# A gated linear attention with an MLP on one core: the start of its hand-kept order table written anew

## The chip, the core and the metric

One core of a Trainium2 chip runs the whole kernel. The metric is the device time of one execution in microseconds (us). The core has five instruction streams that matter here: PE (TensorE, matrix products into PSUM), ACT (ScalarE, table functions and copies), DVE (VectorE, elementwise work), POOL (GpSimd, elementwise work, and issuer of the two weight transfers) and SP (SyncE, issuer of all other transfers). Each stream runs its instructions in the order in which they were written down, and waits where an instruction needs something that isn't there yet.

## The reference

Four batches, eight heads, 768 steps, 48 channels a head. A complex decay per step and channel drives a state; only the real part of the state is read.

```python
mag = np.sqrt(a_re * a_re + a_im * a_im)
scale = np.minimum(mag, 0.999) / (mag + 1e-06)
a_re_n, a_im_n = (a_re * scale, a_im * scale)
for t in range(S):
    new_re = ar * S_re - ai * S_im          # ar, ai: a_re_n, a_im_n of step t
    new_im = ar * S_im + ai * S_re
    kv = np.einsum('bhd,bhe->bhde', k[:, :, t], v[:, :, t])
    S_re, S_im = (new_re + kv, new_im)
    y[:, :, t] = np.einsum('bhd,bhde->bhe', q[:, :, t], S_re)
...
x = np.ascontiguousarray(attn_out.transpose(0, 2, 1, 3)).reshape(B, S, H * D)   # 384 wide
mu = np.mean(x, axis=-1, keepdims=True)
var = np.mean((x - mu) ** 2, axis=-1, keepdims=True)
xn = (x - mu) / np.sqrt(var + 1e-06) * g_ln
ch = np.maximum(xn @ w_ch1, 0.0) @ w_ch2     # 384 -> 1536 -> 384
return (x + ch).astype(np.float32)
```

## The kernel before

**Tiling.** The 768 steps of a batch are cut into 6 chunks of 128 steps. Two chunks form a pair, so there are 12 pairs P (three a batch) and 24 chunks n. Most of what depends on the decays is done by pairs, the attention itself and the layer norm by chunks, the MLP by pairs again. Only pair 0 has its decay work cut into two halves of four heads (`0.0` and `0.1`).

**One pair's steps**, by the names that the table uses (P is the pair, n the chunk, the last figure a half or a chunk within the pair):
- loads on SP: `are`, `aim` (decays, `in_a_re_dram`, `in_a_im_dram`), `k`, `q`, `vf` (values). `v` is the conversion of `vf` (L414).
- magnitude and angle of the decays: `ln` and `iv` on ACT (logarithm and reciprocal, L459, L461), `r` = quotient (L463, a product), `r2` its square (L467), `u` (ACT, L473), `l` and `lc` (DVE, L477 and L480: the capped log magnitude), `th` (ACT, arctangent, L496).
- running sums over the steps by matrix products with triangles of ones: `dec` (L488) for the magnitude, `ph` (L503, L507) for the angle; `car` carries the angle to the next pair; `qt` (L532) adds a quarter turn. From them ACT makes `e` and `en` (exponentials, L492) and `sin` and `cos` (L525, L536 and, later in the table, L548 with `abs` on DVE).
- `ke` = k times en, `qe` = q times e (float32 inputs), then `ks` and `qs` = ke and qe times the sine and cosine. These four are products of two tensors; they are cut in halves when the `.1` half stands in the table, and else the `.0` does the whole 768 (1536 for ks and qs).
- by chunks: `kT`, `qT` transpose on PE (or by a DMA), `ksT`, `qsT` copy out of PSUM; `am` is the score product (L636), `atm` its masking on DVE, `gm` the new part of the state (L660), `G` the state, `y` the attention output in PSUM (L697 and L700).
- layer norm and MLP: `bn` (DVE, L707 and L708), `x` (the centred row, L714 or L717), `xr` (what ot adds, L724), `xtr` and `xT` (transpose on PE, copy), `rstd` (POOL: an addition L753 and a power L755), `mm1` (first layer, L767, three groups of two parts a pair), `relu` (L779), `mm2` (second layer, L791), `ot` (L807), `st` (store).

**Once only.** `wl.0` loads the first layer's weights through POOL's queue, with conversion to bfloat16 (L369); nine `wc.jb.ec` multiply them by minus the norm's gain on DVE (L385), and `mm1.P.jb` needs the three `wc` of its group and both `xT` of its pair. `wl.1` loads the second layer's (L371). Constants (`ue`, `uth`, `pick`, `mask`, `ident`, `pad`, `one` ...) are written at the start; `uec` and `uthc` (L336), which only pairs 9 to 11 use, as well. `warm` are matrix products of constants whose result nobody reads (L821 to L828).

**What sets the order.** Nothing is scheduled by the compiler. The string PLAN (L44 to L142) lists every operation as `name:engine`, and each engine issues in the table's order. A figure behind the engine is the PSUM bank (there are eight); an operation that gets a bank waits until the bank's last owner has been read. An `@name` behind a POOL operation adds a wait: it begins only when the DVE operation of that name has ended (`turns at the shared port` in Graph.run). The tables of ACT's functions are loaded where `tab` stands.

The places around the start, in words: ACT works on the decays of pairs 0 and 1, then makes the sines and cosines of pairs 0 and 1, last cos.1.0. DVE multiplies ke and qe by them in order; qs.1.0.0 is the last of this block. Then come the copies, masks, states and norms of chunks 0 to 3 with the transposes and products of PE between them, the nine `wc`, and `mm1.0.*`.

Of the kernel before, what the change touches and what calls it, by code (L numbers as in the profile page):

```python
# [44 lines left out]
ue:G are.0.0:S are.1.0:S are.0.1:S uth:V aim.0.0:S warm.w27:P0 pad.ks.2:G warm.1:P0 aim.0.1:S pad.qs.2:G warm.w1:P7  # L45
aim.1.0:S warm.w7:P0 tab.log.0:A ln.0.0:A pick:G@uth warm.w29:P5 are.2.0:S iv.0.0:A warm.w32:P0 car0.0:G warm.w10:P7
pad.qs.1:G ln.1.0:A warm.w35:P4 vf.0.0:S uec:G warm.w5:P7 ln.0.1:A pad.qs.0:G warm.22:P2 iv.1.0:A warm.10:P4 r.0.0:V
warm.6:P5 one:G zrow.1:G vf.0.1:S ident:G warm.w24:P5 iv.0.1:A warm.26:P7 warm.w26:P6 r.0.1:V warm.17:P6 gln:S
warm.21:P5 warm.18:P4 r.1.0:V warm.w15:P4 warm.24:P4 q.0.0:S warm.20:P3 warm.w25:P2 tab.trig.1:A th.0.0:A warm.w39:P3
# [5 lines left out]
q.1.0:S car.0.1:V0 en.0.1:A1 r.2.0:V qrow:G warm.w16:P2 en.0.0:A7 ph.1.0:P2 e.1.0:A4 q.2.1:S ke.0.0.0:V e.0.0:A7
warm.28:P1 are.3.0:S r2.2.0:V en.1.0:A4 warm.19:P7 warm.w4:P1 ke.0.1.0:V vf.1.0:S u.2.0:A warm.w0:P5 qe.0.0.0:V
warm.w40:P4 warm.w22:P7 car.1.0:V2 warm.w3:P7 k.1.0:S warm.5:P7 warm.w20:P5 l.2.0:V warm.w31:P7 warm.w23:P5 aim.3.0:S
warm.w21:P7 warm.w28:P1 qe.1.0.0:V tab.trig.3:A sin.0.1:A0 sin.0.0:A6 lc.2.0:V qt.0.1:P0 ks.0.1.1:V sin.1.0:A2 row.0:S
qs.0.1.1:V warm.w2:P7 warm.w19:P4 ks.0.0.1:V row.1:S qt.0.0:P6 qe.1.0.1:V cos.0.1:A0 qt.1.0:P2 vf.1.1:S cos.0.0:A6
# [5 lines left out]
bn.1:V5 decc.0:A4 xtr.0:P4 kT.3:P6 ksT.2:V7 ph.2.0:P2 G.1:V0 qe.2.0.1:G@ksT.2 tab.trig.5:A th.3.0:A ksT.3:V6 am.2:P0
ngl:G@ksT.2 sin.2.0:A2 warm.w37:P7 v.1:G atm.2:V0 warm.13:P7 am.3:P6 xT.0:A4 qt.2.0:P2 r2.3.0:G@ksT.3 x.1:A5 gm.2:P4
atm.3:V6 ph.3.0:P0 cos.2.0:A2 xr.0:G G.2:V4 warm.23:P2 are.5.0:S xtr.1:P2 car.3.0:A0 warm.9:P3 warm.w41:P6 sin.3.0:A0
gm.3:P4 wc.0.1:V y.2:P7 wc.1.0:V y.3:P5 xT.1:A2 wc.1.1:V wc.1.2:V vf.2.0:S qt.3.0:P0 wl.1:G@wc.1.1 bn.2:V7
mm1.0.1.0:P2 cos.3.0:A0 wc.0.0:V mm1.0.1.1:P2 vf.2.1:S wc.0.2:V x.2:A7 wc.2.2:V mm1.0.0.1:P0 wc.2.0:V relu.0.1:A2
wc.2.1:V bn.3:V5 mm1.0.0.0:P0 qe.2.0.0:G@wc.2.1 xtr.2:P3 aim.5.0:S x.3:V5 mm1.0.2.0:P6 ke.2.0.0:G@bn.3 xT.2:V3  # L70
xtr.3:P5 mm1.0.2.1:P6 xT.3:V5 tab.log.6:A u.3.0:A gs.3:V4 mm1.1.0.1:P2 qs.2.0.0:V relu.0.2:A6 mm1.1.1.0:P4 ks.2.0.0:V
relu.0.0:A0 mm1.1.1.1:P4 ks.2.0.1:V mm1.1.0.0:P2 l.3.0:V ln.4.0:A mm1.1.2.1:P0 relu.1.1:A4 relu.1.0:V2 kT.5:P6
mm1.1.2.0:P0 iv.4.0:A ksT.5:V6 qT.5:P4 relu.1.2:A0 lc.3.0:V qT.4:P3 r.4.0:G@ksT.5 qsT.5:V4 kT.4:P5 qsT.4:A3 dec.3.0:P6
ksT.4:V5 are.6.0:S am.5:P0 e.3.0:A6 rstd.0:G am.4:P2 atm.5:V0 r2.4.0:A mm2.0.0:P4 mm2.0.1:P4 atm.4:V2 u.4.0:A q.3.0:S
rstd.1:G@atm.5 mm2.2.0:P1 ln.5.0:A row.3:S mm2.0.2:P4 l.4.0:V q.3.1:S v.2:A mm2.2.1:P1 G.3:G ot.0:V4 mm2.2.2:P1
iv.5.0:A lc.4.0:V k.3.1:S gm.4:P5 en.3.0:A6 dec.4.0:P2 r.5.0:G G.4:V5 y.4:P4 oa.2:A1 st.0:S y.5:P0 bn.4:V4 mm2.3.0:P7
ln.6.0:A k.3.0:S ot.2:G bn.5:V0 mm2.1.0:P6 en.4.0:A2 x.4:V4 mm2.3.1:P7 e.4.0:A2 st.2:S r2.5.0:V vf.3.1:S mm2.1.1:P6
qe.3.0.0:V x.5:A0 row.4:S xtr.4:P2 qe.3.0.1:V iv.6.0:A mm2.3.2:P7 vf.3.0:S xr.3:G@qe.3.0.0 xT.4:V2 xtr.5:P5 u.5.0:A
mm2.1.2:P6 xr.1:G@qe.3.0.1 q.4.0:S xT.5:V5 ke.3.0.1:G ot.3:V7 mm1.2.0.0:P4 ot.1:V6 mm1.2.0.1:P4 aim.6.0:S rstd.2:G
qs.3.0.0:V k.4.0:S mm1.2.2.0:P2 tab.trig.7:A th.4.0:A ke.3.0.0:V mm1.2.2.1:P2 k.4.1:S relu.2.0:A4 ks.3.0.0:V ph.4.0:P6  # L80
st.1:S relu.2.2:A2 st.3:S l.5.0:V qT.6:P0 q.4.1:S abs.4.0:A6 dps.4:P1 kT.6:P5 v.3:G@ks.3.0.0 qsT.6:V0 mm1.2.1.0:P2
are.7.0:S th.5.0:A decc.4:V1 ksT.6:V5 kT.7:P0 sin.4.0:A6 vf.4.0:S dps.3:P4 mm1.2.1.1:P2 decc.3:V4 car.4.0:A6 ksT.7:V0
qT.7:P5 relu.2.1:A2 lc.5.0:V am.6:P6 r.6.0:G@ksT.7 qsT.7:V5 gm.6:P4 ph.5.0:P0 cos.4.0:A atm.6:V6 vf.4.1:S G.6:A4
am.7:P2 sin.5.0:A0 gm.7:P4 q.5.0:S ke.4.0.0:G@atm.6 atm.7:V2 y.6:P5 mm2.4.0:P7 abs.5.0:A0 ke.4.0.1:G mm2.5.0:P6
th.6.0:A G.7:V4 q.5.1:S y.7:P2 bn.6:V5 cos.5.0:A qe.4.0.0:G@G.7 mm2.5.1:P6 are.8.0:S bn.7:V2 x.6:A5 mm2.5.2:P6
aim.7.0:S x.7:V2 mm2.4.1:P7 ks.4.0.0:V k.5.1:S xtr.7:P2 xtr.6:P5 mm2.4.2:P7 tab.log.8:A ln.7.0:A xT.7:V2 ksT.8:S
dec.5.0:P0 xT.6:V5 r2.6.0:A qs.4.0.0:V kT.9:P4 e.5.0:A0 mm1.3.1.0:P2 v.4:G@xT.6 aim.8.0:S ksT.9:V4 en.5.0:A0 qT.8:P5
xr.5:V qe.5.0.0:G qT.9:P4 k.5.0:S qsT.8:V5 u.6.0:A mm1.3.1.1:P2 qsT.9:V4 rstd.3:G mm1.3.2.0:P0 relu.3.1:A2 l.6.0:V
am.9:P4 k.7.1:S mm1.3.2.1:P0 qe.5.0.1:G iv.7.0:A atm.9:V4 mm1.3.0.1:P2 relu.3.2:A0 xr.4:G@qsT.9 mm1.3.0.0:P2 lc.6.0:V
r.7.0:G ot.4:V7 ln.8.0:A dec.6.0:P4 ot.5:V6 relu.3.0:A2 gm.8:P7 st.5:S ph.6.0:P0 G.8:V7 st.4:S qs.5.0.0:V e.6.0:A4  # L90
k.6.1:S am.8:P2 vf.5.0:S mm2.6.0:P6 en.6.0:A4 r2.7.0:G@G.8 abs.6.0:V0 row.6:S mm2.6.1:P6 iv.8.0:A are.9.0:S car.6.0:V0
y.9:P4 atm.8:V2 u.7.0:A r.8.0:G@abs.6.0 qT.11:P5 gm.9:P7 mm2.6.2:P6 k.6.0:S bn.9:V4 y.8:P2 q.6.0:S gs.9:V7 mm2.7.0:P3
xr.6:G tab.trig.9:A sin.6.0:A0 bn.8:V2 G.9:G@gs.9 mm2.7.1:P3 x.9:A4 ot.6:V6 mm2.7.2:P3 x.8:A2 l.7.0:V st.6:S xtr.9:P7
th.7.0:A q.6.1:S qT.10:P4 qsT.11:V5 vf.5.1:S xtr.8:P6 xr.7:G@l.7.0 cos.6.0:A ph.7.0:P0 xT.8:V6 ke.5.0.0:G@qsT.11
xT.9:V7 th.8.0:A qsT.10:V4 dps.6:P2 mm1.4.1.0:P6 sin.7.0:A0 ot.7:V3 mm1.4.0.1:P4 st.7:S rstd.4:G decc.6:A2 ks.5.0.0:V
r2.8.0:A mm1.4.0.0:P4 k.7.0:S vf.6.1:S lc.7.0:V mm1.4.1.1:P6 ke.6.0.0:G relu.4.0:A4 car.7.0:V0 aim.9.0:S kT.10:P3
kT.11:P2 abs.7.0:A0 ksT.10:V3 mm1.4.2.0:P4 relu.4.1:A6 ksT.11:V2 q.7.0:S am.10:P0 ks.6.0.1:V dec.7.0:P2
ks.6.0.0:G@ksT.11 atm.10:V0 q.7.1:S am.11:P6 mm1.4.2.1:P4 atm.11:V6 tab.log.10:A en.7.0:A2 mm2.9.0:P1 v.5:G@atm.10
e.7.0:A2 mm2.9.1:P1 relu.4.2:V4 qe.6.0.0:G@atm.11 ln.9.0:A y.10:P0 row.7:S gm.10:P2 vf.7.0:S ph.8.0:P6 u.8.0:A
# [763 lines left out]
```

## Time and profile before

| | |
|---|---|
| median of 3 runs | 185.67 us (185.29 to 185.86) |
| profiled execution, own time | 185.77 us |
| its span | 184.1 us |
| busy in the span | PE 174.6, DVE 154.6, ACT 154.9, POOL 111.4 us |
| HBM | 28.31 MB read, 4.72 MB written, 179 GB/s over the span |

The profile is one execution. The span runs from the first instruction to the last; the execution's own time is 1.7 us longer, which lies around the span. PE busy means that matrix products are in flight, fillers among them. A timeline row gives start, duration, engine, line, operation, and output and input with their shapes; "x3" means that three instructions alike stand in one row, with the time of all three. A bracket gives the idle time ahead of it on its engine and who ended it. A row of the chain gives start, duration and what ran. A row of the table of stages gives the stretch, its length, and the busy time and count of each engine. "PEclk" is the granted clock of PE as a share of full speed, "DMA share" the mean busy share of the sixteen transfer engines.

### The profile page before, as it was taken

To read this page: it belongs to the slowest core of one execution; us is meant where nothing else is said; L and a number is where in the kernel's file an instruction comes from. 1 tells how busy PE (TensorE), PEld (TensorE's weight loads), DVE (VectorE), ACT (ScalarE), POOL (GpSimd) and SP (SyncE) were. 2 spreads that over 40 slices of the span, in tenths; PEclk is the share of its full clock that TensorE was granted. 3 is DMA by queue.
4 is the path that set the end of the run, shared out by engine and by line. 5 is a ranking of instruction groups with operands and counts; after the bars stand their busy time and mean duration, and the time that the engine had idled before them with its cause. 6 is when DMAs were issued, how large, how long until landed. Compare 5 with 4: busy or idle time off the path is not lost.

```text
span 184.1 us, 5013 instructions
## 1 busy us (share of the span) xinstructions
PE 174.6 (95%) x1971; PEld 137.8 (75%) x1971; DVE 154.6 (84%) x274; ACT 154.9 (84%) x217; POOL 111.4 (61%) x124
## 2 busy tenths in 40 slices
...
GB/s 156 306 195 240 231 194 198 197 246 207 241 178 149 263 244 228 210 204 198 184 239 155 253 203 217 221 171 196 151 199 177 200 152 190 230 184 89 109 0 85
DMA packets 128791, 35.39 MB, mean 192 GB/s; under 512 B 124800, under 2 KB 128000, under 8 KB 128768
## 3 DMA queue, kind: packets, MB, share of 16 engines
...
q8 instruction: 15, 0.25, 0.5%
...
HBM read 28.31 MB, written 4.72 MB: 179 GB/s over the span
## 4 chain that ended last, share of the span: by engine, by line
PE 74%; DVE 9%; SPq 6%; POOL 4%; issue 3%; DMA 2%; DVEq 0%; POOLq 0%
PE banks L767 24%; PE banks L791 24%; PE banks L613 6%; PE banks L636 5%; SPq L452 3%; PE banks L488 3%; PE banks L507 3%; PE banks L697 2%; DMA k<-in_k_dram 2%; SPq L404 2%; PE banks L660 2%; PE banks L700 2%; PE banks L734 2%; POOL ke L295 2%; PE banks L503 1%
## 5 line engine op out<-in xcount | busy, mean ns | idle before, releaser
L791 PE MATMUL banks<-w2b,h 128*128 128x384 bf16 (+2 forms) x300 | 53.0, 319 | 0.1
L767 PE MATMUL banks<-xT,w1b 128*128 128x256 bf16 x432 | 51.5, 273 | 0.0
L767 PEld LDWEIGHTS <-w1b 128*128 128x128 bf16 x432 | 46.1, 114 | 1.2 <-DVE stats L707 0.3
L779 ACT ACTIVATE h<-banks 128x1024 bf16<-128x1024 f32 x31 | 31.5, 1022 | 11.7 <-PE banks L767 11.3
L791 PEld LDWEIGHTS <-h 128*128 128x128 bf16 x300 | 26.9, 97 | 13.9 <-issue 0.2
L295 DVE TENSOR_TENSOR atm<-banks,mask 128x1024 bf16<-128x1024 f32 x24 | 28.9, 1220 | 3.5 <-PE banks L636 3.0
L295 POOL TENSOR_TENSOR r<-aim,are 128x768 f16<-128x768 f32 x9 | 16.5, 1832 | 8.6 <-DVE ksT L292 7.5
L831 ACT ACT_TABLE_LOAD x15 | 19.2, 1283 | 1.0 <-PEq L847 0.8
L295 POOL TENSOR_TENSOR qe<-q,e 128x384 bf16<-128x384 f32 (+1 forms) x14 | 16.2, 1156 | 4.7 <-ACT e L492 1.7
L826 PE MATMUL banks<-u_e 128*128 128x512 f16 x42 | 14.1, 424 | 2.4 <-POOL u_e L323 2.2
L724 POOL TENSOR_SCALAR xr<-x,mv 128x384 f32<-128x384 bf16 x13 | 8.5, 658 | 11.0 <-ACT x L714 4.5
L707 DVE BATCH_NORM_STATS2 stats<-banks 128x6 f32<-128x384 f32 x24 | 13.4, 556 | 1.4 <-PE banks L700 1.2
L636 PE MATMUL banks<-qsT,ksT 128*128 128x128 bf16 x192 | 14.3, 219 | 0.0
L807 DVE SCALAR_TENSOR_TENSOR ot<-banks,rstd,xr 128x384 f32<-128x384 f32 (+2 forms) x18 | 10.4, 587 | 3.9 <-PE banks L791 3.3
L477 DVE SCALAR_TENSOR_TENSOR l<-r,w 128x768 f16<-128x768 f16 (+1 forms) x13 | 11.7, 908 | 2.3 <-ACT r L473 2.3
L636 PEld LDWEIGHTS <-ksT 128*128 128x128 bf16 x192 | 12.2, 98 | 1.6 <-DVE ksT L292 0.2
L414 POOL TENSOR_SCALAR v<-vf 128x768 bf16<-128x768 f32 x9 | 9.5, 1061 | 5.6 <-DVE mv L708 2.7
L805 POOL TENSOR_TENSOR ot<-ot,x 128x384 f32<-128x384 f32 x7 | 7.1, 1007 | 9.1 <-DVE atm L295 7.9
L697 PE MATMUL banks<-v,atm 128*128 128x48 bf16 x192 | 12.0, 183 | 0.2 <-DVE atm L295 0.2
L295 POOL TENSOR_TENSOR ke<-k,en 128x768 bf16<-128x768 f32 (+1 forms) x9 | 11.9, 1324 | 0.2
L459 ACT ACTIVATE w<-are 128x768 f32<-128x768 f32 (+1 forms) x13 | 10.2, 791 | 2.1 <-DMA are<-in_a_re_dram 2.1
L697 PEld LDWEIGHTS <-atm 128*128 128x128 bf16 x192 | 10.7, 96 | 1.4 <-DVE atm L295 0.6
...
## 6 DMA issues: line engine op xcount, KB each, us to landing
...
```

What stands on the lines that cost most here:

```text
L295: {"DVE": nc.vector, "POOL": nc.gpsimd}[eng(name)].tensor_tensor(**kw)
L477: nc.vector.scalar_tensor_tensor(out=S_("l"), in0=S_("r2"), scalar=0.5, in1=S_("w"), op0=ALU.mult, op1=ALU.add)
L613: nc.tensor.transpose(ps[:, h], T(nm, P)[:, c, h], ident)
L636: nc.tensor.matmul(ps[:, h], lhsT=T("ksT", n)[:, h], rhs=T("qsT", n)[:, h], start=True, stop=True)
L697: nc.tensor.matmul(ps[:, h], lhsT=T("atm", n)[:, h], rhs=T("v", P)[:, c, h], start=True, stop=nfirst)
L707: nc.vector.bn_stats(out=T("stats", n), in_=bank(f"y.{n}")[:, 0:DM])
L767: nc.tensor.matmul(ps[:, jj], lhsT=w1b[:, dc, ts(gi, JG * C)].rearrange("k (p j) -> k j p", j=JG)[:, jj], rhs=T("xT", P)[:, dc].rearrange( ...
L779: act(out=dst, in_=src, func=AF.Relu)
L791: nc.tensor.matmul(bank(f"o.{N}")[:, ws], lhsT=T("h", P)[:, j, ts(c, C)], rhs=w2b[:, j, ws], start=(j == 0), stop=(j == NJ - 1))
L807: nc.vector.scalar_tensor_tensor(out=o, in0=bank(f"o.{N}")[:, ws], scalar=T("rstd", P)[:, ds(c, 1)], in1=xs, op0=ALU.mult, op1=ALU.add)
L826: g.add(f"warm.w{i}", lambda i=i: nc.tensor.matmul(bank(f"warm.w{i}"), lhsT=u_e[:, 0, 0], rhs=u_e.rearrange("p c j t -> p (c j t)"), start ...
L831: g.add(f"tab.{nm}.{i}", lambda tab=tab: nc.scalar.preload_act_table_set(tab))
```

## The change

Two things: the counts of the fillers (29 and 42 become 8 and 56), and the table. The rows ahead of the first layers of pairs 0 and 1 stand in another order on all engines. Behind about `kT.5` the order on each engine is that of before, but for `uthc`, `uec`, `one` and `xr.0`, which stand later than they did. Many `@` of POOL name another operation, or are gone, along the whole table: before, they name DVE operations of any kind, copies out of PSUM among them; after, only such as work in SBUF alone (l, lc, ks, qs, ke, qe, xr, wc).

Three products are on another engine: `r2.0.1` DVE to POOL, `r2.1.0` POOL to DVE, `qe.0.1.0` POOL to DVE. Three halves are merged into one operation (`qe.1`, `qe.2`, `ks.2`), one is cut in two (`ke.2`).

The core of the diff (rows shortened to the operations named here; "..." stands for the rest of the table):

```diff
 # the sines and cosines of pairs 0 and 1, and what follows from them on DVE
-... sin.0.1:A0 sin.0.0:A6 lc.2.0:V qt.0.1:P0 ks.0.1.1:V sin.1.0:A2 row.0:S qs.0.1.1:V ... ks.0.0.1:V row.1:S
-... qe.1.0.1:V cos.0.1:A0 ... cos.0.0:A6 ks.0.1.0:V dec.2.0:P0 qs.0.1.0:V cos.1.0:A2 ks.0.0.0:V k.2.1:S
-qs.0.0.0:V qs.0.0.1:V ... th.2.0:A qs.1.0.0:V qT.0:P6 ... wl.0:G@qs.0.0.1 kT.1:P3 ksT.0:V4 ... k.2.0:S qsT.0:V6
-ke.1.0.0:G q.2.0:S tab.log.4:A ... are.4.0:S ksT.1:V3 qsT.1:A5 atm.0:V6 ks.1.0.0:G
+... sin.0.1:A7 sin.0.0:A6 vf.1.1:S qt.0.1:P7 lc.2.0:V sin.1.0:A2 ... qs.0.1.1:V qs.0.0.1:V ... cos.0.1:A7 ks.0.0.1:V
+qt.1.0:P2 ks.0.1.1:V cos.0.0:A6 qs.0.1.0:V cos.1.0:A2 ks.0.1.0:V k.2.0:S qs.0.0.0:V ks.0.0.0:V qT.0:P5 ... qs.1.0.0:V
+... gm.0:P0 th.2.0:A kT.0:P3 q.2.0:S qsT.0:V5 qT.1:P7 wl.0:G@qs.1.0.0 G.0:A0 kT.1:P4 ksT.0:V3 qsT.1:A7 gm.1:P0
+k.2.1:S ke.1.0.0:G@qs.1.0.0 ... ks.1.0.0:G
 # weights and first layer
-G.2:V4 ... wc.0.1:V y.2:P7 wc.1.0:V y.3:P5 xT.1:A2 wc.1.1:V wc.1.2:V ... wl.1:G@wc.1.1 bn.2:V7 mm1.0.1.0:P2 cos.3.0:A0
-wc.0.0:V mm1.0.1.1:P2 wc.0.2:V x.2:A7 wc.2.2:V mm1.0.0.1:P0 wc.2.0:V relu.0.1:A2 wc.2.1:V bn.3:V5 mm1.0.0.0:P0
-qe.2.0.0:G@wc.2.1 xtr.2:P3 x.3:V5 mm1.0.2.0:P6 ke.2.0.0:G@bn.3 xT.2:V3 xtr.3:P5 mm1.0.2.1:P6
+G.2:V4 ... wc.2.1:V xtr.1:P2 wc.1.1:V y.3:P5 sin.3.0:A0 wc.1.0:V gm.3:P4 wc.1.2:V wc.0.2:V xT.1:A2 qt.3.0:P0 wc.0.1:V
+wc.0.0:V mm1.0.1.1:P2 cos.3.0:A0 bn.2:V6 wl.1:G@wc.0.0 mm1.0.1.0:P2 wc.2.2:V x.2:A6 mm1.0.0.0:P0 wc.2.0:V relu.0.1:A2
+bn.3:V5 ke.2.0.1:G@wc.2.0 mm1.0.2.0:P6 x.3:V5 xtr.2:P2 qe.2.0.0:G@wc.2.0 mm1.0.0.1:P0 xT.2:V2 gs.3:V4 xtr.3:P2
+mm1.0.2.1:P6
 # POOL behind the first layers of pairs 0 and 1
-r.4.0:G@ksT.5 ... rstd.0:G ... rstd.1:G@atm.5
+r.4.0:G@lc.3.0 ... xr.0:G ... one:G uec:G ... rstd.0:G ... rstd.1:G
 # one stretch of the later table, with the moved uthc
-xT.6:V5 r2.6.0:A qs.4.0.0:V kT.9:P4 ... v.4:G@xT.6 ... ksT.9:V4 ... xr.5:V qe.5.0.0:G ... qsT.8:V5 ... qsT.9:V4
-rstd.3:G ... l.6.0:V am.9:P4 ... qe.5.0.1:G ... atm.9:V4 ... xr.4:G@qsT.9 ... lc.6.0:V r.7.0:G ot.4:V7 ... gm.8:P7
-... qs.5.0.0:V ... r2.7.0:G@G.8
+xT.6:V5 ... qs.4.0.0:V r2.6.0:A ... v.4:G@qs.4.0.0 ksT.9:V4 ... uthc:V ... xr.5:V ... qsT.8:V5 ... qe.5.0.0:G@xr.5
+... qsT.9:V4 ... rstd.3:G@xr.5 ... l.6.0:V am.9:P4 ... atm.9:V4 qe.5.0.1:G@l.6.0 ... xr.4:G@l.6.0 ... lc.6.0:V
+... ot.4:V7 ... r.7.0:G@lc.6.0 ... gm.8:P7 ... qs.5.0.0:V ... r2.7.0:G@qs.5.0.0
...
-    for i in range(29):
+    for i in range(8):
         g.add(f"warm.{i}", ...)
-    for i in range(42):
+    for i in range(56):
         g.add(f"warm.w{i}", ...)
```

193 lines of the change are left out of this document (96 added, 97 removed).

## The prediction

> **What bounds the kernel now.** I read the page's shares of busy time first, then a table of stages (busy time of each engine in five stretches of the span), then the chain that ended last.
>
> ```profile
> span 184.1 us, 5013 instructions
> ...
> PE 174.6 (95%) x1971; PEld 137.8 (75%) x1971; DVE 154.6 (84%) x274; ACT 154.9 (84%) x217; POOL 111.4 (61%) x124
> ...
> PE 74%; DVE 9%; SPq 6%; POOL 4%; issue 3%; DMA 2%; DVEq 0%; POOLq 0%
> ```
> ```profile
> core 0: us, PE busy (x) PEld busy (x) DVE busy (x) ACT busy (x) POOL busy (x), PEclk, DMA share, GB/s
> 8.90:23.30 14.40, 11.58 (x71) 6.02 (x69) 11.82 (x29) 14.33 (x25) 5.94 (x10) 1.00 1.07 222
> 23.30:38.00 14.70, 13.84 (x221) 10.99 (x222) 14.20 (x27) 13.44 (x22) 11.98 (x10) 1.00 0.95 192
> 38.00:80.00 42.00, 42.00 (x470) 35.38 (x470) 38.22 (x72) 40.69 (x52) 27.45 (x28) 1.00 1.03 223
> 80.00:96.00 16.00, 16.00 (x193) 12.80 (x191) 14.88 (x26) 15.68 (x22) 13.94 (x11) 1.00 0.91 200
> 96.00:180.00 84.00, 83.94 (x989) 68.78 (x987) 72.00 (x121) 64.74 (x92) 46.47 (x47) 1.00 0.88 171
> ```
> ```profile
> 38.05 2.74 PE banks L767 x24
> ```
> From 38.00 to 180.00 TensorE is busy 141.94 of 142.00 us; the chain's first layer of pair 0 (L767) begins at 38.05. So the end is set by when that layer starts, by TensorE's work behind it, which the diff leaves alone, and by any gap that a new wait tears into it. Ahead of 38, TensorE is padded with filler matmuls, and others decide: ACT is full (14.33 of 14.40) to 23.3, then VectorE (14.20 of 14.70). The granted clock is 1.00 in every stretch; fewer fillers come before 38 and stay dense, and I cost them at nothing.
>
> What decides 38, from the timelines and the table of transfers:
>
> ```profile
> 21.62 1.60 ACT L536 ACTIVATE trig<-banks 128x384 bf16<-128x384 int16 x3
> 23.22 1.49 DVE L295 TENSOR_TENSOR qs<-qe,trig 128x384 bf16<-128x384 bf16 x3
> 24.15 1.00 POOL L369 DMA_DIRECT2D w1b<-in_moe_w_ch_dram  x1 [7.81 <-DMA row<-e]
> w1b<-in_moe_w_ch_dram POOLq DMA_DIRECT2D x1, 1152.0 KB, 12.0
> 35.84 0.55 DVE L295 TENSOR_TENSOR G<-banks,G 128x384 bf16<-128x384 f32 x1
> 36.31 1.13 DVE L385 TENSOR_SCALAR w1b<-w1b,ngl 128x512 bf16<-128x512 bf16 x4
> 37.35 0.56 DVE L707 BATCH_NORM_STATS2 stats<-banks 128x6 f32<-128x384 f32 x1
> 37.95 0.18 DVE L708 BATCH_NORM_AGGREGATE mv<-stats 128x2 f32<-128x6 f32 x1
> 38.80 0.57 ACT L714 ACTIVATE x<-banks,mv 128x384 bf16<-128x384 f32 x1
> 39.52 1.02 ACT L779 ACTIVATE h<-banks 128x1024 bf16<-128x1024 f32 x1
> 41.62 1.15 PE L767 MATMUL banks<-xT,w1b 128*128 128x256 bf16 x9
> ```
> The first weights (wl.0) are issued at 24.15, behind qs.0.0.1, and land 12.0 later, about 36.15. Their scaling on VectorE (wc) starts at 36.31, when G.2 is also just out of the way: weights and VectorE arrive together.
>
> **The change part by part, stage 1 (to the first layer).** ACT issues the same set of instructions up to cos.1.0, with the same table loads (u.0.0 only comes ahead of one), and was full; so cos.1.0 still ends near 21.62 + 1.60 = 23.2. New is that wl.0 waits for qs.1.0.0, the one product of 768 that needs cos.1.0. I price it at the 0.95 of a qs of that size (row at 73.84 below): it ends at 24.1, and with the 0.3 that separates release and issue before, wl.0 goes out at 24.4, 0.25 late, landing at 36.4 by the same 12.0. Behind the waiting wl.0 on POOL stand only ke.1.0.0 and its successors, which the same wait holds.
>
> VectorE is earlier: before, the last ks/qs ends at 23.22 + 1.49 = 24.71, now at 24.1; the same copies, masks and G follow, so G.2 ends by 36.39 − 0.6 = 35.8, and up to 0.5 sooner if the stretch's idle time (14.70 − 14.20) closes. That gain is covered by the weights. Then 7 scalings run ahead of bn.2 instead of 4 (1.13 / 4, overlapped some 0.265 each: 1.86), bn.2 0.77, x.2 0.57, relu.0.1 1.02; only then is bank 2 free for xtr.2 (it had bank 3), behind it 6 matmuls and xtr.3. With hand-overs of some 0.1, the seventh product of the layer (mm1.0.2.1) starts at landing + 5.4, about 41.8; before it starts at 41.62. **Term: +0.2**, bounded by −0.8 (VectorE decides, weights early) and +1.2 (weights a us later, below).
>
> The three moved products: r2.0.1 goes to POOL at about half of the 1.46 below, and is done before ACT has finished the table load that precedes u.0.1; r2.1.0 and qe.0.1.0 go to VectorE, which has 2.6 us of slack before 23.3. The merged qe.1.0.0 saves VectorE 0.1, the merged qe.2.0.0 and ks.2.0.0 and the split ke.2 fall where POOL is idle or after 38 behind TensorE's queue. All nothing; if that slack were gone, up to 0.5 would enter through qs.1.0.0. On SP, are.4.0 and gln only trade places with q loads; k.2.0 and q.2.0 now go ahead of wl.0, k.2.1 behind it. They share the transfer engines with the weights (share 0.95): nothing, or up to 1 us of delay.
>
> **Stage 2 (POOL's turns, 74 to 82 us).** Behind 47 us the order is the old one but for uthc, now on VectorE ahead of xr.5, and for POOL's turns: they pointed at any VectorE operation and now only at those that touch no PSUM.
>
> ```profile
> 73.84 0.95 DVE L295 TENSOR_TENSOR qs<-qe,trig 128x1536 bf16<-128x1536 bf16 x1
> 75.50 0.41 DVE L724 TENSOR_SCALAR xr<-x,mv 128x384 f32<-128x384 bf16 x1
> 76.00 1.29 DVE L292 COPY qsT<-banks 128x1024 bf16<-128x1024 bf16 x2
> 77.20 0.95 DVE L477 SCALAR_TENSOR_TENSOR l<-r,w 128x768 f16<-128x768 f16 x1
> 79.65 1.12 DVE L807 SCALAR_TENSOR_TENSOR ot<-banks,rstd,xr 128x384 f32<-128x384 f32 x2
> ```
> ```profile
> 74.01 1.47 POOL L414 TENSOR_SCALAR v<-vf 128x768 bf16<-128x768 f32 x1 [1.77 <-DVE xT L292]
> 75.55 1.14 POOL L295 TENSOR_TENSOR qe<-q,e 128x384 bf16<-128x384 f32 x1
> 76.76 0.22 POOL L753 TENSOR_SCALAR rstd<-mv 128x2 f32<-128x2 f32 x1
> 77.06 0.71 POOL L755 TENSOR_TENSOR rstd<-rstd,half_n 128x2 f32<-128x2 f32 x1
> 77.74 1.20 POOL L295 TENSOR_TENSOR qe<-q,e 128x384 bf16<-128x384 f32 x1
> 78.93 0.58 POOL L724 TENSOR_SCALAR xr<-x,mv 128x384 f32<-128x384 bf16 x1
> 81.72 2.05 POOL L295 TENSOR_TENSOR r<-r 128x768 f16<-128x768 f16 x1 [0.31 <-DVE G L295]
> ```
> ```profile
> 11.54 0.83 POOL L414 TENSOR_SCALAR v<-vf 128x768 bf16<-128x768 f32 x1
> 39.55 0.91 POOL L295 TENSOR_TENSOR qe<-q,e 128x384 bf16<-128x384 f32 x1 [1.23 <-DVE w1b L385]
> 34.37 1.46 POOL L295 TENSOR_TENSOR r<-r 128x768 f16<-128x768 f16 x1
> 116.37 0.95 DVE L477 SCALAR_TENSOR_TENSOR l<-r,w 128x768 f16<-128x768 f16 x1
> 116.46 1.42 POOL L755 TENSOR_TENSOR rstd<-rstd,half_n 128x2 f32<-128x2 f32 x1
> L336 DVE TENSOR_SCALAR u_thc<-u_ec x1: 478/478/478, 9.7 to 9.7; 128x256 f16<-128x256 f16 x1
> 80.61 0.36 PE L660 MATMUL banks<-v,ks 128*128 128x48 bf16 x8
> ```
> v.4 ran from 74.01, beside qs.4.0.0, in 1.47 where a lone v takes 0.83. Now it waits for that qs: 74.88 to 75.71 instead of 75.48. qe.5.0.0 gets a wait for xr.5, which uthc (0.48) pushes from an end of 75.91 to 76.3; at the lone 0.91 it ends at 77.3 (before 76.69). So rstd.3's addition is at 77.4 and its power at 77.7, no longer ahead of l.6.0 but inside it (77.4 to 78.35). The nearest row for that is rstd.6: its power, issued 0.09 after an l began, took 1.42 instead of 0.71. Then it ends at 79.1, qe.5.0.1 at 80.1, xr.4 at 80.7, and ot.4, which needs xr.4, starts at 80.8 instead of 79.65. ot.4 (0.56) must empty bank 7 for gm.8, on TensorE at 80.61: now 81.4. **Term: +0.8**. Lower bound +0.1, with the power at 0.71: then qe.5.0.1 waits for l.6.0 alone (78.45 to 79.4), xr.4 ends at 80.0 and gm.8 is 0.1 late; no gain, as TensorE had no idle time here. Upper bound +1.1, all of ot.4's delay. Fillers are gone by then and TensorE is in order, so nothing covers this.
>
> A rule of the Trainium skill speaks to this ("GPSIMD Engine Reference", section 8, key points): the two engines share their SBUF interfaces and contend in VectorE's two-port mode or with two SBUF inputs. The 1.47 against 0.83 and the 1.42 against 0.71 agree; by it, turns that ignore PSUM operations are the right ones, and the price is only where a turn now comes late, as above.
>
> **Stage 3 and the rest.** r.7.0 and r2.7.0 follow on POOL, about 1 late; u.7.0 behind r2.7.0 holds ACT, but TensorE is 0.8 late itself: **+0.1** (0 to 0.25; r2.7.0 alone after qs.5.0.0 may take 1.46 instead of 2.05, which pays part of it). The other turns later than 96 move by less than POOL's idle time (46.47 busy of 84.00): 0, between −0.2 and +0.3. one, uec, xr.0 and the rstd behind them come to POOL at about 49 instead of ahead; ot.0 and y.5 could wait 0.1: taken as 0.
>
> **Sum.** 0.2 + 0.8 + 0.1 = +1.1. The profiled execution took 185.77, so 186.9 on its own time; the median of the runs is 185.67, 0.1 lower: **186.8**.
>
> **Rivals.**
> Rival 1, the weights land a us or more sooner. Two hw loads that stood beside wl.0 go ahead of it, and 12.0 is long for 1152 KB when the core moves 192 GB/s (a lone 1152 KB at that rate takes 6.1). If they land by 35.4, G.2 on VectorE decides, stage 1 gives −0.8 instead of +0.2, and the time is 185.8: no change. Against it: the transfer share is 0.95, as full as before. The Trainium skill ("DMA: Bandwidth & Descriptors", section "Anatomy of one DMA — SWDGE (gpsimd) path") gives such a transfer some 2.0 us and its bytes at 436 GB/s, an estimate of 4.7; by that rule wl.0 would be home at 29 and rival 1 would be certain. The trace's 12.0 says otherwise.
> Rival 2, the power isn't held. Its start would be some 0.3 into l.6.0, not 0.09, and my times for it are good to 0.3: ended before l.6.0 begins (77.4), or passed by, the term is +0.1 and the time is 186.1, within 0.3% of before.
> Rival 3, both of these, the one on the other side: 185.67 − 0.8 + 0.1 + 0.1, about 185.0, faster. The one that decides the sign is the landing: with rival 2 given, each 0.1 that the weights come ahead of 36.2 is a gain, to G.2's end.
> Rival 4, weights a us later: k.2.0 and q.2.0 take the share that wl.0 had. 187.8.
>
> **How the numbers follow.** Forecast 0.36, rival 1 0.20, rival 2 0.17, rival 3 0.15, rival 4 0.12. A measurement of this kernel tells about 0.3% (0.56 us) from no change, so faster is below 185.1, slower above 186.2. Rival 3 lies about that edge and rival 1 can fall below it when VectorE's idle closes: faster 0.22. Rivals 1 and 2 mostly: same 0.30. Forecast, rival 4 and the upper half of rival 2: slower 0.48. The range reaches from 184.8 (rival 3, with the 0.2 of the later turns) to 187.8 (rival 4), as both signs carry weight; the likeliest case alone is 186.1 to 187.2.
>
> **What the profile after would show.** Right: wl.0 issued near 24.4 and first wc near 36.5; xtr.2 behind relu.0.1; v.4 at 0.83; rstd.3's power at about 1.4; ot.4 near 80.9 plus stage 1's shift; a TensorE gap of about 0.8 before gm.8. Wrong: a first wc before 35.8 with G.2 as its releaser (rivals 1 and 3), a power of 0.71 and no gap at gm.8 (rival 2). What would overturn it all is a cause that I have at nothing: ACT no longer full before 23.2, or a gap of TensorE behind 96.

## The result and the profile after

The changed kernel takes 186.5 us (median of 14 runs, 186.11 to 188.38) against 185.68 (14 runs, 185.16 to 185.86): a ratio of 1.0062, 95% interval 1.004 to 1.0085. It is 0.8 us slower. The profile kept of it comes from the longest of the 14 executions, 188.38 us; a second one of the same kernel, of 186.99 us, is shown with the first experiment.

The page of that profile, first the span, the busy shares and the chain by engine, then one row of its costliest groups, and behind them two rows of the table of stages:

```profile
span 186.7 us, 4998 instructions
...
PE 177.4 (95%) x1964; PEld 136.8 (73%) x1964; DVE 157.6 (84%) x273; ACT 155.4 (83%) x217; POOL 103.2 (55%) x123
...
PE 63%; DMA 12%; ACT 8%; DVE 5%; issue 5%; POOL 4%; SPq 1%; POOLq 0%; DVEq 0%
...
L790 PE MATMUL banks<-w2b,h 128*128 128x384 bf16 (+2 forms) x300 | 53.0, 319 | 1.7 <-DMA w2b<-in_moe_w_ch_dram 1.7
```
```profile
38.00:80.00 42.00, 40.27 (x451) 33.35 (x451) 36.80 (x69) 39.09 (x49) 23.77 (x28) 1.00 1.00 214
80.00:96.00 16.00, 15.50 (x179) 11.95 (x177) 14.70 (x26) 14.66 (x22) 13.53 (x14) 1.00 0.93 205
```
TensorE has gaps now where it had none: 1.73 us between 38 and 80, 0.50 between 80 and 96. (Behind the changed part all line numbers are one lower: L791 is L790.) The chain, 74% TensorE's before, is its for 63% only, with 12% of transfers in it instead of 2%.

The timelines of the start, to be laid beside those of before. First, what the second layer's weights and its first product (mm2.0.0) did before:

```profile
37.48 0.84 POOL L371 DMA_DIRECT2D w2b<-in_moe_w_ch_dram  x1 [1.08 <-DVE w1b L385]
w2b<-in_moe_w_ch_dram POOLq DMA_DIRECT2D x1, 1152.0 KB, 10.6
49.53 4.06 PE L791 MATMUL banks<-w2b,h 128*128 128x384 bf16 x24
```
And now:

```profile
22.20 1.60 ACT L535 ACTIVATE trig<-banks 128x384 bf16<-128x384 int16 x3
23.99 0.95 DVE L294 TENSOR_TENSOR qs<-qe,trig 128x1536 bf16<-128x1536 bf16 x1
25.25 1.00 POOL L368 DMA_DIRECT2D w1b<-in_moe_w_ch_dram  x1 [12.37 <-DVE qs L294]
36.04 0.55 DVE L294 TENSOR_TENSOR G<-banks,G 128x384 bf16<-128x384 f32 x1
36.51 1.92 DVE L384 TENSOR_SCALAR w1b<-w1b,ngl 128x512 bf16<-128x512 bf16 x7
38.74 0.83 POOL L370 DMA_DIRECT2D w2b<-in_moe_w_ch_dram  x1 [2.62 <-DVE w1b L384]
51.55 4.06 PE L790 MATMUL banks<-w2b,h 128*128 128x384 bf16 x24 [1.73 <-DMA w2b<-in_moe_w_ch_dram]
```
and from the table of transfers, with the us from issue to landing at the end:
```profile
w1b<-in_moe_w_ch_dram POOLq DMA_DIRECT2D x1, 1152.0 KB, 9.5
w2b<-in_moe_w_ch_dram POOLq DMA_DIRECT2D x1, 1152.0 KB, 12.8
```
The first weights are home at 34.7 and wait for VectorE, whose G.2 ends at 36.59 (36.39 before). The second weights go out at 38.74 (37.48 before) and land at 51.5; TensorE stands 1.73 us for them, and mm2.0.0 starts at 51.55 instead of 49.53.

The stretch that was at 74 to 82 us, here 2.0 later. Two rows of before, lc.6.0 on VectorE and r.7.0 on POOL, belong to it:

```profile
79.34 0.39 DVE L480 TENSOR_SCALAR l<-l 128x768 f16<-128x768 f16 x1
79.49 1.92 POOL L295 TENSOR_TENSOR r<-aim,are 128x768 f16<-128x768 f32 x1
```
POOL, VectorE and TensorE of the changed kernel:

```profile
76.95 0.83 POOL L413 TENSOR_SCALAR v<-vf 128x768 bf16<-128x768 f32 x1 [2.85 <-PE banks L612]
78.33 0.92 POOL L294 TENSOR_TENSOR qe<-q,e 128x384 bf16<-128x384 f32 x1 [0.54 <-ACT en L491]
79.31 1.02 POOL L752 TENSOR_SCALAR rstd<-mv 128x2 f32<-128x2 f32 x1
80.41 0.71 POOL L754 TENSOR_TENSOR rstd<-rstd,half_n 128x2 f32<-128x2 f32 x1
81.99 0.68 POOL L723 TENSOR_SCALAR xr<-x,mv 128x384 f32<-128x384 bf16 x1
```
```profile
77.52 0.34 DVE L335 TENSOR_SCALAR u_thc<-u_ec 128x256 f16<-128x256 f16 x1
79.31 0.94 DVE L476 SCALAR_TENSOR_TENSOR l<-r,w 128x768 f16<-128x768 f16 x1
81.36 0.86 DVE L479 TENSOR_SCALAR l<-l 128x768 f16<-128x768 f16 x1
82.70 1.14 DVE L806 SCALAR_TENSOR_TENSOR ot<-banks,rstd,xr 128x384 f32<-128x384 f32 x2 [0.48 <-POOL xr L723]
```
```profile
82.27 0.81 PE L487 MATMUL banks<-l,u_e 128*128 128x384 f16 x4
83.37 0.36 PE L659 MATMUL banks<-v,ks 128*128 128x48 bf16 x8 [0.29 <-DVE ot L806]
```
rstd.3's addition starts with l.6.0 and takes 1.02 instead of 0.22; xr.4 and ot.4 are 1.0 later than the 2.0 of shift, and gm.8 (L659) waits for ot.4. Ahead of that dec.6.0 (L487) is 0.3 late, behind an lc.6.0 that took 0.86 instead of 0.39. That adds nothing to the loss: gm.8 would stand behind ot.4 all the same.

To compare executions whose starts differ by some tenths, two marks of TensorE's timeline serve from here on: the start of mm2.0.0, and the distance from the start of mm2.3.0 to that of gm.8, within which TensorE has the same work in the same order in all kernels.

| kernel | median us (runs), ratio to before | mm2.0.0 | mm2.3.0 to gm.8 |
|---|---|---|---|
| before | 185.68 (14) | 49.53 | 55.10 to 80.61: 25.51 |
| changed (marks: its long execution) | 186.5 (14), 1.0062 | 51.55 | 57.11 to 83.37: 26.26 |
| e1 changed again | 186.63 (6), 1.0049 (1.003 to 1.0067) | 49.71 | 55.26 to 81.53: 26.27 |
| e2 second weights earlier | 186.96 (6), 1.0070 (1.005 to 1.0089) | 49.38 | 55.11 to 81.49: 26.38 |
| e3 old waits, uthc at 77 | 187.90 (5), 1.0125 (1.0105 to 1.0144) | 49.26 | 54.97 to 82.30: 27.33 |
| e4 new waits, uthc later | 186.26 (9), 1.0047 (1.002 to 1.0074) | 49.34 | 55.07 to 80.95: 25.88 |
| e5 old waits, uthc later | 186.08 (12), without its longest 1.0016 (0.9997 to 1.0035) | 52.17 | 57.73 to 83.24: 25.51 |
| e6 before, uthc at 77 | 187.16 (4), 1.0079 (1.0057 to 1.0101) | 49.05 | 54.61 to 81.94: 27.33 |
| e7 before, second weights late | 188.65 (4), 1.0182 (1.0142 to 1.0221) | 52.80 | 59.96 to 85.48: 25.52 |
| e8 e5, second weights earlier | 185.75 (10), 1.0005 (0.9985 to 1.0025) | 49.21 | 54.94 to 80.46: 25.52 |
| e9 e8, xr.0 earlier | 185.88 (12), 1.0014 (0.9992 to 1.0036) | 49.07 | 54.74 to 80.26: 25.52 |
| e10 before, seven new waits | 187.31 (4), 1.0078 (1.0053 to 1.0103) | 49.92 | 55.48 to 81.36: 25.88 |
| e11 changed, first weights earlier | 191.97 and 188.3 (2) | 54.69 | 60.42 to 86.72: 26.30 |
| e12 before, six new waits | 186.45 (12), 1.0036 (1.0019 to 1.0053) | 50.10 | 55.66 to 81.54: 25.88 |

The start itself is read with care. The five executions whose table has the old start (before, e6, e7, e10, e12; e6 without uthc in it) have cos.1.0's end from 22.84 to 23.76 and the first transpose behind the first layers, kT.5, from 45.06 to 46.11. Most of this comes in with the first loads: ACT's logarithm of are.1.0 starts at 4.86 to 5.78, and from there to the end of cos.1.0 it is 18.0 to 18.25 us. A difference of some tenths between two single executions says nothing there.

### The profile page after: what moved, and what is told of

It reads as the page before. It is cut to its first block, busy times and chain, and to the rows that moved or that the text cites. A ratio compares the mean times of both kernels' runs of the same rounds, so it can differ in the third digit from the quotient of the medians.

```text
span 186.7 us, 4998 instructions
## 1 busy us (share of the span) xinstructions
PE 177.4 (95%) x1964; PEld 136.8 (73%) x1964; DVE 157.6 (84%) x273; ACT 155.4 (83%) x217; POOL 103.2 (55%) x123
## 4 chain that ended last, share of the span: by engine, by line
PE 63%; DMA 12%; ACT 8%; DVE 5%; issue 5%; POOL 4%; SPq 1%; POOLq 0%; DVEq 0%
PE banks L790 23%; PE banks L766 19%; DMA w2b<-in_moe_w_ch_dram 7%; PE banks L612 4%; PE banks L635 4%; DMA aim<-in_a_im_dram 3%; POOL r L294 3%; DMA are<-in_a_re_dram 2%; PE banks L506 2%; PE banks L487 2%; PE banks L696 2%; ACT L830 2%; PE banks L699 2%; PE banks L659 2%; PE banks L733 1%
## 5 line engine op out<-in xcount | busy, mean ns | idle before, releaser
L790 PE MATMUL banks<-w2b,h 128*128 128x384 bf16 (+2 forms) x300 | 53.0, 319 | 1.7 <-DMA w2b<-in_moe_w_ch_dram 1.7
L766 PE MATMUL banks<-xT,w1b 128*128 128x256 bf16 x432 | 51.5, 273 | 0.0
L790 PEld LDWEIGHTS <-h 128*128 128x128 bf16 x300 | 26.9, 97 | 15.5 <-issue 1.9
L825 PE MATMUL banks<-u_e 128*128 128x512 f16 x56 | 16.5, 437 | 2.2 <-POOL u_e L322 2.2
L294 POOL TENSOR_TENSOR qe<-q,e 128x384 bf16<-128x384 f32 (+1 forms) x12 | 13.9, 1161 | 4.2 <-ACT h L778 1.6
L723 POOL TENSOR_SCALAR xr<-x,mv 128x384 f32<-128x384 bf16 x13 | 7.7, 593 | 10.2 <-DVE stats L706 5.3
L413 POOL TENSOR_SCALAR v<-vf 128x768 bf16<-128x768 f32 x9 | 8.0, 894 | 8.9 <-DVE ks L294 3.3
L825 PEld LDWEIGHTS <-u_e 128*128 128x128 f16 x56 | 5.9, 109 | 9.6 <-issue 4.4
L294 POOL TENSOR_TENSOR ke<-k,en 128x384 bf16<-128x384 f32 (+1 forms) x10 | 12.1, 1211 | 0.5 <-DVE w1b L384 0.4
L291 DVE COPY ksT<-banks 128x1024 bf16<-128x1024 bf16 x16 | 10.7, 685 | 1.6 <-PE banks L612 1.2
```

What stands on the lines that cost most here:

```text
L291: nc.vector.tensor_copy(out=dst, in_=src)
L294: {"DVE": nc.vector, "POOL": nc.gpsimd}[eng(name)].tensor_tensor(**kw)
L766: nc.tensor.matmul(ps[:, jj], lhsT=w1b[:, dc, ts(gi, JG * C)].rearrange("k (p j) -> k j p", j=JG)[:, jj], rhs=T("xT", P)[:, dc].rearrange( ...
L790: nc.tensor.matmul(bank(f"o.{N}")[:, ws], lhsT=T("h", P)[:, j, ts(c, C)], rhs=w2b[:, j, ws], start=(j == 0), stop=(j == NJ - 1))
L825: g.add(f"warm.w{i}", lambda i=i: nc.tensor.matmul(bank(f"warm.w{i}"), lhsT=u_e[:, 0, 0], rhs=u_e.rearrange("p c j t -> p (c j t)"), start ...
```

## The experiments

The theory after the two traces: three places, the start (0.1), the turns of POOL (0.7), and the second weights (a tail). The rival: the second weights are all of it.

**e1: the changed kernel again**, no edit.

> The changed kernel once more, unedited. The theory (three places): its first layer of pair 0 is 0.1 us late, the turns of POOL at 74 to 82 us cost 0.7 us of TensorE's time, and the second layer's weights land about when their first product is due (49.7 us), so that they cost nothing in most executions and 1 to 2 us in a few. Then a typical execution takes 186.3 to 186.6 us, its profile shows little or no wait of L790 for w2b and again a gap before gm.8 near 81 us. The rival (the weights are all of it): the wait for w2b is in every execution at 0.5 to 1 us and the loss behind 74 us is made up later.

```profile
49.71 4.06 PE L790 MATMUL banks<-w2b,h 128*128 128x384 bf16 x24 [0.30 <-DMA w2b<-in_moe_w_ch_dram]
81.53 0.36 PE L659 MATMUL banks<-v,ks 128*128 128x48 bf16 x8 [0.29 <-DVE ot L806]
```
186.63 us. The wait for the second weights is 0.30 here and was 1.73 in the long execution; the gap before gm.8 is the same 0.29, and the distance between the marks 26.27 against 25.51. So 0.76 us is lost between the marks whatever the weights do; in the long execution the weights add their wait. The start, though, was not late but 0.3 early (kT.5 at 45.26, before at 45.55).

**e2: the second weights as early as before.**
```diff
-wl.1:G@wc.0.0
+wl.1:G@wc.1.1
```


> One edit to the changed kernel: the load of the second layer's weights waits for wc.1.1, not for wc.0.0, so it goes out near 37.4 us as in the kernel before, instead of 38.7. By the three places: no execution near 188, the median within 0.3 us of the changed kernel's usual 186.4, the gap before gm.8 unchanged. By the rival (the weights are all of it): back to the time before, 185.7.

The profile has no wait for w2b and mm2.0.0 starts at 49.38, yet the median is 186.96, no better than e1's. The rival falls: without any wait for the weights the loss of 0.87 between the marks is all there. Its profile shows in part why it isn't 0.3 faster than e1: mm2.0.0 is 0.33 ahead of e1's, but mm2.3.0 only 0.15, because G.4 waits for POOL (see e8), and 0.11 more goes between the marks. The intervals of the two overlap. What the earlier issue does change is the tail: of the 46 runs with the late issue (changed, e1, e3, e4, e5) five are 1.4 us or more above the median of their row, of the 28 with the changed start and the early issue (e2, e8, e9) none is more than 1.0 above. Two of the five have a profile, and both wait 1.7 us for these weights.

**e3: seven waits as before, uthc where the change put it.**
```diff
-v.4:G@qs.4.0.0 qe.5.0.0:G@xr.5 rstd.3:G@xr.5 qe.5.0.1:G@l.6.0 xr.4:G@l.6.0 r.7.0:G@lc.6.0 r2.7.0:G@qs.5.0.0
+v.4:G@xT.6 qe.5.0.0:G rstd.3:G qe.5.0.1:G xr.4:G@qsT.9 r.7.0:G r2.7.0:G@G.8
```


> Seven waits of POOL of the stretch from 74 to 82 us are put back as they were (v.4, qe.5.0.0, rstd.3, qe.5.0.1, xr.4, r.7.0, r2.7.0); uthc stays at 77 us. By the three places: xr.4 no longer late, no gap before gm.8, dec.6.0 not behind lc.6.0, and 0.6 to 0.8 us faster than the changed kernel (185.7 to 185.9 where the weights are in time). By the rival: no change.

```profile
75.42 0.95 POOL L294 TENSOR_TENSOR qe<-q,e 128x384 bf16<-128x384 f32 x1
79.57 1.81 POOL L294 TENSOR_TENSOR r<-aim,are 128x768 f16<-128x768 f32 x1
```
```profile
75.37 0.22 DVE L335 TENSOR_SCALAR u_thc<-u_ec 128x256 f16<-128x256 f16 x1
75.51 1.07 DVE L723 TENSOR_SCALAR xr<-x,mv 128x384 f32<-128x384 bf16 x1
80.20 1.40 DVE L479 TENSOR_SCALAR l<-l 128x768 f16<-128x768 f16 x1
```
```profile
81.65 0.81 PE L487 MATMUL banks<-l,u_e 128*128 128x384 f16 x4 [1.25 <-DVE l L479]
```
187.90: slower by 1.3, not faster by 0.7. The theory that the waits are the cost falls. What is seen is that xr.5 takes 1.07 where it took 0.41, and lc.6.0 1.40 where it took 0.39. Before, xr.5 began at 75.50, 0.05 ahead of qe.5.0.0, and it was qe.5.0.0 that ran long (1.14). Here uthc (0.22) stands ahead of xr.5; qe.5.0.0 is first by 0.09 and runs in 0.95, and xr.5 is the long one. The same with r.7.0 and lc.6.0 four microseconds on: lc.6.0 begins behind r.7.0 instead of ahead of it. That gave the second theory, first come, other held: of a POOL and a VectorE instruction that both work in SBUF, the one that begins second is stretched until the other is done. VectorE feeds TensorE here, so it matters which.

**e4: uthc alone to a later place.**
```diff
-uthc:V aim.8.0:S xr.5:V
+aim.8.0:S xr.5:V
...
-ks.5.0.0:V
+ks.5.0.0:V uthc:V
```


> uthc alone is moved on VectorE, from ahead of xr.5 to behind ks.5.0.0; all waits stay. xr.5 ends 0.3 us sooner, so qe.5.0.0 does, and rstd.3's addition comes 0.1 to 0.2 us before l.6.0 begins instead of with it. If what begins inside l is held until it ends and what begins before is not, the addition takes 0.22 instead of 1.02, the power falls inside l and takes 1.4, and xr.4 is 0.0 to 0.3 us earlier: 0 to 0.2 us faster than the changed kernel. If uthc is the whole trigger, xr.4 is on time and it is 0.6 us faster.

```profile
77.08 0.22 POOL L752 TENSOR_SCALAR rstd<-mv 128x2 f32<-128x2 f32 x1
77.38 1.31 POOL L754 TENSOR_TENSOR rstd<-rstd,half_n 128x2 f32<-128x2 f32 x1
```
The addition is ahead of l.6.0 and takes 0.22; the power falls inside l.6.0 (77.17 to 78.12) and takes 1.31. lc.6.0 is 0.48. The loss between the marks falls from 0.76 to 0.37. The median is 186.26, with two runs of nine at 187.7. The held instruction is as expected. The gain of 0.39 has two halves: the addition begins 0.19 sooner than in e1, as uthc no longer stands ahead of xr.5, and from its start to the end of the power it is 1.61 us instead of 1.80. dec.6.0, no longer late, has no part in it: here as in the changed kernel gm.8 is late by what ot.4 is late (0.66, there 1.04) less 0.29.

**e5: both edits, e3's and e4's.**

> The changed kernel with both edits of the second and third experiment of this study's first four together: the seven waits from 74 to 82 us as before, and uthc behind ks.5.0.0. Singly they gave +1.3 us (waits) and -0.4 us (uthc) in the medians. The theory (first come, other held): of a VectorE and a POOL instruction that both work in SBUF alone, the one that starts second is held; in the old order VectorE is first each time, and uthc ahead of xr.5 makes POOL first. Then the two edits together give the old stretch: no TensorE gap between 74 and 82 us, xr.5 and lc.6.0 at 0.4 us, and 185.4 to 185.8 us (0.2 for the earlier start, and the second weights late in some executions). The rival (the effects add): 186.4 + 1.3 - 0.4, about 187.3.

Between the marks 25.51, as before, so the effects don't add: the old waits are harmless without uthc (0.00), and cost 1.82 with it (e3). The median is 186.08; the profile fell on its longest execution (188.32), in which mm2.0.0 waits 1.69 for the second weights, as in the long one of the changed kernel. Here the first weights were late as well:
```profile
36.50 2.58 DVE L384 TENSOR_SCALAR w1b<-w1b,ngl 128x512 bf16<-128x512 bf16 x7 [0.53 <-DMA w1b<-in_moe_w_ch_dram]
```
The scalings start 0.53 late, one of them begins beside a ke on POOL and takes 1.0, and the second weights, which wait for the seventh, go out at 39.40 (38.3 to 38.7 in the changed kernel, e1, e3 and e4).

**e6: the kernel before with uthc moved to 77 us**, nothing else.
```diff
-r2.0.1:V uthc:V
+r2.0.1:V
...
-qT.8:P5
+qT.8:P5 uthc:V
```


> The kernel before with one token moved: uthc from its start to ahead of xr.5, as in the changed kernel; every wait as before. By first come, other held: xr.5 begins after qe.5.0.0 and is held (1.0 us instead of 0.41), l.6.0 after qe.5.0.1 (1.4 instead of 0.95), lc.6.0 inside r.7.0 (1.4 instead of 0.39); dec.6.0 waits for lc.6.0, a TensorE gap of 1.2 to 1.5 us near 80, and 187.0 to 187.4 us. If uthc costs only its own 0.2 to 0.5 us, and VectorE's slack takes it: 185.7 to 186.0.

```profile
75.15 1.08 DVE L724 TENSOR_SCALAR xr<-x,mv 128x384 f32<-128x384 bf16 x1
77.34 1.44 DVE L477 SCALAR_TENSOR_TENSOR l<-r,w 128x768 f16<-128x768 f16 x1
79.84 1.40 DVE L480 TENSOR_SCALAR l<-l 128x768 f16<-128x768 f16 x1
81.29 0.81 PE L488 MATMUL banks<-l,u_e 128*128 128x384 f16 x4 [1.25 <-DVE l L480]
```
187.16, in the expected range, with the expected lengths and gap. One instruction of 0.22 us on an engine that had slack costs 1.4 us of time, 1.82 between the marks (the profiled execution had started 0.5 early).

**e7: the kernel before with the second weights sent late.**
```diff
-wl.1:G@wc.1.1
...
-bn.3:V5
+bn.3:V5 wl.1:G@bn.3
```


> The kernel before with the second layer's weights sent 2.8 us later (behind bn.3, near 40.3 us, instead of behind wc.1.1 at 37.5); nothing else. By the account of the tail: with 10.6 to 12.8 us to landing they come at 50.9 to 53.1, their first product is due at 49.5, so TensorE waits 1.4 to 3.6 us for them and the median is 187.0 to 189.3. If the landing is not set by the issue but by the queues ahead (transfers sent later land sooner after issue), it is under 0.5 us.

The product that waits, from its timeline, and two rows of its table of stages (the granted clock is the third figure from the end):
```profile
52.80 5.66 PE L791 MATMUL banks<-w2b,h 128*128 128x384 bf16 x24 [2.12 <-DMA w2b<-in_moe_w_ch_dram]
```
```profile
50.00:54.00 4.00, 1.88 (x15) 1.05 (x13) 3.31 (x4) 3.65 (x6) 3.66 (x6) 0.83 0.67 132
54.00:58.00 4.00, 4.00 (x20) 2.13 (x19) 0.72 (x2) 1.47 (x3) 2.06 (x2) 0.74 0.19 39
```
188.65 (188.55 to 190.56, 4 runs; ratio 1.0182, 1.0142 to 1.0221), in the range. In the profiled one (190.56) the weights take 12.0 us and the wait is 2.12, and the granted clock then falls (0.83 and 0.74 as means of the two stretches), so that the 24 products take 5.66 instead of 4.06. The issue is 3.3 us later (40.77 for 37.48) and the transfer 1.4 longer than in the profile of before, so the landing is 4.7 later; the reserve of 1.4 that was there pays for a part, and mm2.0.0 is 3.3 late (52.80 for 49.53). Transfers sent later don't land sooner after their issue. The other three runs are 1.9 us shorter than the profiled one, with a mean granted clock of 0.996 to 1.00 for its 0.991, so the slower products aren't the rule here.

**e8: e5 and the second weights as early as before.**

> As the kernel with the seven waits and uthc put back, and the second layer's weights behind wc.1.1 as well (issue near 37.5). By the three places every cost is undone: 185.3 to 185.7 us with no execution above 186.2. In the first four runs the earlier issue alone gave 187.0 against 186.6 without a cause in the profile; if that is real, this one is 0.3 us slower than the one without it.

185.75. No wait for w2b, nothing lost between the marks, and two runs of ten above 186.2 (186.64, 186.71), where none was expected. With these three edits undone, the rest of the change, the rewritten start and the other moved waits, costs nothing that the medians show. The early start of 0.32 at mm2.0.0 is 0.16 at mm2.3.0:
```profile
53.95 0.56 DVE L294 TENSOR_TENSOR G<-banks,G 128x384 bf16<-128x384 f32 x1 [0.90 <-POOL G L294]
```
G.4 waits for G.3 on POOL, which xr.0, one and uec ahead of rstd.0 push back from an end of 53.27 to 53.92.

**e9: and xr.0, one and uec out of the way.**
```diff
-xr.0:G ... one:G uec:G
...
+relu.1.0:V2 xr.0:G@qs.2.0.0 one:G uec:G
```


> The kernel with three places undone (seven waits, uthc, the second weights' issue), and a fourth: xr.0, one and uec, which held up rstd.0 and G.3 on POOL at 49 us, go to POOL's idle time behind qs.2.0.0 near 44 us. In the last profile G.4 waited 0.9 us for G.3, and y.5 was 0.16 us late by it. By that account G.4 has no wait for POOL, TensorE keeps the 0.3 us that the new start is ahead through to the end, and the time is 185.2 to 185.5 us, a little below both kernels. If xr.0 beside the norm and the scalings holds VectorE, it is 0.2 to 0.5 us slower than without this edit (185.75).

G.4 no longer waits for POOL, gm.8 starts at 80.26 (before 80.61), and the span is 183.5 us, the shortest of the profiled ones. But the runs fall into two groups, six at 185.24 to 185.65 and six at 186.1 to 186.88, and the median, 185.88, is no better than before's: the expected 185.2 to 185.5 isn't shown. What parts the groups stays open: the profile is of the first.

**e10: the kernel before with the seven new waits**, uthc at the start.

> The kernel before with the changed kernel's seven waits from 74 to 82 us, and uthc at the start where it was: the fourth corner of the square of waits and uthc. By first come, other held, VectorE stays the first everywhere and POOL pays: the power of rstd.3 inside l.6.0 takes 1.3 us, xr.4 is 0.7 us late, gm.8 waits 0.2 to 0.4 us behind ot.4, and the time is 186.0 to 186.2 us. If the waits cost only in company with uthc: 185.7.

Between the marks it loses 0.37, as in e4, with the power of rstd.3 at 1.31, lc.6.0 at 0.48, and with VectorE idle for 0.48 ahead of ot.4, which waits for xr.4. That was expected; the time, 187.31, was not. Its execution started 0.4 late, another 0.2 came near 93 us, and 0.4 more behind 160 us, in a part of the table that the edit leaves alone.

**e12: six of the seven**, r2.7.0 behind G.8 as before.
```diff
-r2.7.0:G@qs.5.0.0
+r2.7.0:G@G.8
```


> The kernel before with six of the seven waits: r2.7.0 waits for G.8 as before, not for qs.5.0.0. The run with all seven took 187.3, 1.2 more than its gap at 81 us explains (0.4 there; its start was 0.4 later in the profiled execution, and 0.2 more came at 93 us, behind a u.7.0 that was 0.4 later than TensorE). If that 0.2 comes from r2.7.0's wait, u.7.0 is 0.3 us earlier here and the shift at 93 us is no larger than at 82. If the late start was chance, the median falls to 186.0 to 186.5; if the waits themselves carry it, it stays at 187.0 to 187.4.

186.45. The late start was chance (0.56 in this profile too, and the runs reach from 185.98 to 187.66), the 0.37 between the marks is there, and u.7.0 is 0.07 behind TensorE's shift instead of 0.36, with no further loss at 93 us. So the last of the seven waits costs about 0.2 on its own through ACT. The medians of e10 and e12 are 0.86 apart; what makes the rest of it in e10's four runs stays open.

**e11: the first weights earlier.**
```diff
-wl.0:G@qs.1.0.0
+wl.0:G@qs.0.0.1
```


> The changed kernel with the first layer's weights behind qs.0.0.1 again, so that they go out near 22.8 us instead of 24.9 and land near 33. By the profiles so far (weights at 34.5 to 36, G.2 out at 36.0 to 36.6) VectorE decides when the scalings start: the first wc right behind G.2 as now, mm1.0.0.0 unchanged within 0.15 us. If the weights decide in the usual execution, the first layer is 0.3 us or more earlier.

Two runs, 191.97 (profiled) and 188.3. POOL's timeline, TensorE's, VectorE's, and two rows of the table of stages:
```profile
33.56 1.81 POOL L294 TENSOR_TENSOR r<-aim,are 128x768 f16<-128x768 f32 x1 [3.33 <-ACT trig L524]
...
36.30 0.80 PE L506 MATMUL banks<-th,u_th 128*128 128x384 f16 x2 [1.82 <-ACT th L495]
...
35.62 3.68 DVE L384 TENSOR_SCALAR w1b<-w1b,ngl 128x512 bf16<-128x512 bf16 x7
```
```profile
34.00:38.00 4.00, 2.12 (x13) 0.96 (x10) 4.00 (x6) 2.02 (x3) 3.75 (x3) 0.69 0.96 220
38.00:42.00 4.00, 4.00 (x53) 2.92 (x52) 3.89 (x12) 2.90 (x5) 1.96 (x3) 0.50 1.08 259
```
Neither expectation holds: the scalings begin right behind G.2 (35.62), but the first layer is 2.7 us later than in the changed kernel (40.66 for 38.00). The weights (issued at 22.37) now start 0.6 us behind aim.3.0 instead of 2.85. The longest landing of any aim load in this trace is 11.7 us, which from aim.3.0's issue at 21.76 makes 33.5; the median of these loads is 3.6. r.3.0 starts right then, 1.7 us later than in the changed kernel, and th.3.0 behind it, TensorE stands 1.82 us, and the granted clock goes to 0.50. The late r2.3.0 on POOL (35.45 to 36.92) then lies beside the scalings, which take 3.68 instead of 1.92. If the weights are what held that load up, the wait that seems only to delay them also keeps them off the loads of pair 3; with one profile and two runs, neither that nor what is usual here is shown.

## Why the prediction was right, and where it wasn't

The time, 186.5 for 186.8, lies well inside the range, and slower was the likeliest sign. By its steps:

- **Stage 1, forecast +0.2, measured +0.1 in the long execution and -0.15 to -0.3 in e1 to e4 against the one profile of before, which is inside the spread of the old start.** Counted from the end of cos.1.0, which takes that spread out, kT.5 comes after 22.2 to 22.4 us with the old start and after 21.8 to 22.2 with the new one; only in e5, with the weights late, after 23.2. So the start gains up to 0.5. ACT was as forecast: cos.1.0 ends at 23.0 to 23.5 in e1 to e4 (forecast 23.2), and at 23.80 in the long execution, where are.1.0 landed 0.45 later; u.0.0 ahead of the table load costs about 0.1. Wrong was the price of the transfer. The 12.0 of before was the longest of five: with the same start the weights take 9.8 to 10.5 in e6, e7, e10 and e12 and are home 1.7 to 2.4 us ahead of G.2's end, so that weights and VectorE arrive together only in the execution that the forecast was read from. With the new start they take 9.4 to 11.8; the scalings waited for them in e1 (by 0.26) and in e5 (0.53), in the other six executions for VectorE. Rival 1 had this mechanism, but not its size: its -0.8 asks for a G.2 that ends near 35.4, and it ends at 35.8 to 36.3 in e1 to e4.
- **Stage 2, forecast +0.8 (0.1 to 1.1), measured 0.75 and 0.76.** Right in place and size: xr.4 and ot.4 some 1.0 late, gm.8 behind ot.4's bank. Held was the addition (1.02), not the power; so rival 2, that the power isn't held, held for the power and did not bring its time. The two come to the same: whichever is held goes on when l.6.0 is done, and without the shift of 2.0 the power ends at 79.1, xr.4 at 80.7 and ot.4 starts at 80.7, as forecast (79.1, 80.7, 80.8). Wrong was the share of the two edits: the prediction charged the waits and gave uthc its 0.48. The runs show uthc at that place costing 1.82 with the old waits, the new waits 0.37 without uthc, and both 0.76: given where uthc went, the new waits saved 1.06.
- **Stage 3, +0.1:** about 0.2 by r2.7.0's wait (e10 against e12), within the stated 0 to 0.25; in e1 TensorE is 0.29 later at 94 us than at gm.8, and 0.15 behind 103. Another 0.13 is lost near 160 us, in e8 and e9 too; it lies within the -0.2 to +0.3 that the forecast gave the later turns.
- **one, uec and xr.0, taken as 0 with 0.1 named:** 0.16, through the G.3 and G.4 that the sentence should have followed.
- **wl.1, left out.** The change makes it wait for wc.0.0, 1.26 us more, and I never priced it, though the profile of before had the landing (37.48 + 10.6 = 48.1) and the due time, 49.5: a reserve of 1.4 us. Measured with that issue: no waiting in e3 and e4, 0.30 in e1, 1.69 in e5, and 1.73 in the execution of 188.38 us; the second run of that length (188.29) has no profile. So it costs a tail, and little in the median. That the sum came within 0.3 of the measured time is in part luck: the stage 1 term had the wrong sign, and this unpriced one and the 0.13 near 160 us stood in for it.

The Trainium skill's rule on the shared interfaces ("GPSIMD Engine Reference", section 8) points to the right pairs: every stretched instruction above overlaps one of the other engine in SBUF. That section doesn't say who pays; e3 and e6 do, with xr.5 at 1.07 and 1.08 behind a qe.5.0.0 of 0.95. The Trainium skill's fit for such a transfer ("DMA: Bandwidth & Descriptors", section "Anatomy of one DMA — SWDGE (gpsimd) path"; 4.7 us by my estimate from it) isn't borne out in any run: the first weights took 9.4 to 12.0.
